# Who makes the second step addition: GpSimd in every bundle of the current round, and the instruction order laid down anew

## The chip, the cores and the metric

The kernel runs on one core of one Trainium2 chip. The metric is the time of one execution in device microseconds (us). The kernel before took 698.04 us as the median of three runs (697.25 to 698.42). The execution that the profiler recorded took 698.16 us; from its first to its last instruction, which is called the span, it is 696.4 us, at a granted TensorE clock of 1.000.

## The reference, cut to what matters

Two attention blocks work on the same input `x` (2048 rows, 512 columns), and a gate for each row mixes them. Block A is softmax attention with 32 heads of 16 columns; block B is linear attention.

```python
q, k, v = qkv[0], qkv[1], qkv[2]                       # block A, per head
scores = jnp.einsum("bhqd,bhkd->bhqk", q, k) * (Dh ** -0.5)
p = _softmax(scores, axis=-1)
o = jnp.einsum("bhqk,bhkd->bhqd", p, v)
...
phi = lambda t: jnp.where(t > 0, t + 1, jnp.exp(t)) + 1e-6   # block B
...
return g * a + (1 - g) * b                             # g = sigmoid((x * gate_w).sum(-1))
```

What costs is the exponential of block A: 32 heads x 2048 x 2048 scores.

## The kernel before, in words

**Units and rounds.** The scores are cut into units of 128 keys x 512 queries of one head; a unit fills one PSUM bank (128 x 512 float32). One round is a set of four heads and one block of 512 queries: 64 units. There are 32 rounds, so 2048 units in all. Each head set's K, V and Q projections, block B, and the output products are cut into steps that are spread between the rounds.

**Two ways to the exponential.** Most units go to ScalarE (`ACTIVATE`, L1999), which takes two or three neighbouring banks at a time (a *group*) and writes bf16 to the tile `PT`. The others are *claimed* for VectorE: L1536 turns the score into an int16 whose bits, read as a float16, are a coarse power of two (tile `DP`). Four claimed units make a *bundle*. A bundle is sharpened by a sum of three such powers, shifted by steps of 0, 342 and 683 in the int16: so each bundle needs two *step additions* over 128 x 2048 int16, from one `DP` buffer to another. VectorE makes them in L1585. For some bundles GpSimd makes the second one instead (L1578, as 128 x 1024 int32 with a pair of step values in each word). The condition stands in `try_close`: the bundle's number must divide by `EVERY`, all of its units must lie in the round that ScalarE is at (`act_round`), the round must not be the last, and over `POOL_LEFT` = 22 of the round's units must not have been claimed. GpSimd also makes the normalisation of most head blocks (`OT`, L1265).

**Products.** TensorE makes the products with V in sets of four matmuls of 32 columns each. A unit on ScalarE is one product (`PT,Vaug`); a bundle of VectorE is twelve (`DP,Vaug`, four units x three shifts).

**What sets the order.** Nothing is scheduled on the chip. A Python loop (`while True:`, with `g` as the number of the group) lays down the order of every engine's instructions once, with clocks of its own for each engine (`PE.t`, `AC.t`, `DV.t`, `PO.t`), estimated durations (`d_act`, `d_sb`, `d_psum`, `POOL_ADD` = 1.97) and constants such as `OVER`, `STARVE`, `LEND`. Every engine then runs its own queue in order, and waits at semaphores. For each group the loop takes two or three units from `next_unit`; if it takes two, the third bank of the slot may carry a claimed unit (`claim_in_group`), so that three score matmuls are issued together. Then it fills TensorE's time until the next group with products (`pv_step`), with projection or output steps (`misc_step`), with claims that stand alone, or with *fills* (`warm`, matmuls on zeros that only keep TensorE busy). VectorE's and GpSimd's pending work is kept in `items` and is laid down by `pump` and `pool_go`. In `est_start` the loop keeps a VectorE operation that reads no PSUM out of the estimated running time of a GpSimd operation (`pool_runs`).

**Banks.** PSUM has eight banks. Banks 0 to 2 and 3 to 5 are two slots (`SLOTS`) in which the groups alternate, bank 6 or 7 holds the accumulator of the products, and the other one (`MISC`) the steps. A third bank of a slot can be lent to a step when the steps are far behind (`LEND`, `lent`).

Lines that the prediction speaks of: L664 (every matmul is recorded under this helper's line), L948 (exponential of block B on ScalarE), L1277 (VectorE copies the accumulator out at a round's end), L1250 (reciprocal of the row sums, which waits for a DMA), L1293 and L1294 (the last round's normalisation).

Of the kernel before, what the change touches and what calls it, by code (L numbers as in the profile page):

```python
# [212 lines left out]
def bass_gated_mix__mha_block__linear_attn_block__prompt_kernel(  # L213
# [29 lines left out]
    PRE_T = 5  # L243
    PRE_GAP = 6
    OUT_GAP = 8

    with ExitStack() as es:
# [193 lines left out]
        POOL_ADD = 1.97  # L441
        EVERY = 2
        POOL_LEFT = 22
# [219 lines left out]
        def f_mm(o, l, r, start=True, stop=True, sg=False):  # L663
            return lambda: nc.tensor.matmul(o, lhsT=l, rhs=r, start=start, stop=stop, skip_group_check=sg)  # L664
# [824 lines left out]
        MIN_LEFT = 14  # L1489
        MIN_LEFT_LAST = 20  # L1490

# [59 lines left out]

        LAZY = 1
        MOST_ADDS = 20
        MOST_OPEN = 0
        CLAIM_FREE_OPEN = 2

        def try_close():

            while closing:
# [7 lines left out]
                if len(free) < (LAZY if early else 1):  # L1567
                    return False
                if not zs and sum(1 for it in items if it.prio == 3) >= (1 if early else MOST_ADDS):
                    return False  # L1570
# [144 lines left out]
        def behind_by():  # L1715

            return max([cur_g[0] - ch[0].target for ch in chains if ch] or [0])
# [23 lines left out]
        def misc_step(now, t_late):  # L1741
# [9 lines left out]
            if b is None:  # L1751
                return False
            due, load = due_step(now)
# [12 lines left out]
        def fill(now):  # L1766
# [17 lines left out]
            return True  # L1784

        HURRY = 40
        CLAIM_FREE = 2
        FORCE_N = 1
        MOST = 3
        OVER = 0.15  # L1790
        FIRST_T = 0.43
        ROOM = 0.4
        CLAIM_LOAD = 3.7
        LATE_CLAIM = 4
        STARVE = 6.0
        MAC_LOW = 0.45
# [141 lines left out]
        while True:  # L1938
# [7 lines left out]
            if g > last_stage and lent[0] is None and hold[0] is None and (behind_by() > LEND or (e_chain and LEND_E)) and bank_free(PE.t + 0.3) is None:  # L1946
                due, _ = due_step(PE.t + 0.3)
                if due is not None and not due[0].keeps:
                    lend = due
            while len(us) < SLOTS[g % 2][1]:  # L1950
                if len(us) == 2 and (away or lend is not None):
                    break
                if len(us) == 2 and g > last_stage:
                    extra = claim_in_group(PE.t, [j for j in range(4) if j not in [u % 4 for _, u in us]])
                    if extra is not None:
                        break
                u = next_unit()
                if u is None:
                    break
                us.append(u)  # L1960
# [31 lines left out]
            pe_macro(fns, reads=rd, writes=[r_bank[b0 + k] for k in range(len(fns))], dur=QK_T, mac=0.053 * len(fns), mode="rows")  # L1992
            if extra is not None:
                claim(extra[0], extra[1], b0 + 2, True, in_group=True)
# [18 lines left out]
            nb0, nbn = SLOTS[(g + 1) % 2]  # L2013
            if lent[0] == nb0 + 2:
                nbn = 2
# [269 lines left out]
```

## Time and profile before

| | |
|---|---|
| runs | 698.04 us, median of 3 (697.25 to 698.42) |
| profiled execution | 698.16 us; span 696.4 us |
| ScalarE busy | 682.6 us in 707 instructions |
| TensorE busy | 672.9 us in 8162 matmuls |
| VectorE busy | 641.6 us in 1099 instructions |
| GpSimd busy | 139.6 us in 91 instructions |

A busy share is how much of the span at least one instruction of that engine was on record. Consecutive instructions of an engine overlap in the record: the next starts while the one before still drains. So a wait that is shorter than the drain doesn't show as idle time, and what one more instruction costs is the distance from start to start, not its recorded duration. In a row of groups, `xcount | busy, mean ns of one | idle before` follow the operation, its tiles and its shape; behind the arrow stands what ended the idle time.

### The profile page before, as it was taken

The numbers are of one execution on the slowest core, as the hardware profiler recorded it, in microseconds if no ns is written. First come the engines' busy times: TensorE is split into PE (matmuls) and PEld (weight loads), VectorE is DVE, ScalarE is ACT, GpSimd is POOL, SyncE is SP. The second block draws the span as 40 slices with busy tenths as digits, with TensorE's granted clock in tenths as the row PEclk, the third lists the DMA queues.
The fourth block names the chain that finished last, engine by engine and source line by source line (L and its number), as shares of the span: only waits on it lengthen the run. The fifth ranks groups of instructions, "written<-read, shape, count | busy, mean of one in ns | idle before, by whom it ended". The sixth has DMA issues, their size and how long they took to land.

```text
span 696.4 us, 19208 instructions
## 1 busy us (share of the span) xinstructions
PE 672.9 (97%) x8162; PEld 203.7 (29%) x8164; DVE 641.6 (92%) x1099; ACT 682.6 (98%) x707; POOL 139.6 (20%) x91
## 2 busy tenths in 40 slices
PE   8999999999999999999999999999999999999997
PEld 4322223232223222333222323323222322222223
DVE  4699999999999999988999999999999999999894
ACT  6999999999999999999999999999999999999996
POOL 4012122121122231112211212232212320312200
PEclk9999999999999999999999999999999999999999
DMA  9800001000010001201001020010211121010121
GB/s 228 230 3 15 20 2 33 2 19 18 5 30 2 18 18 38 52 5 34 2 10 25 19 38 10 17 26 4 46 17 28 38 41 48 9 41 17 26 48 34
DMA packets 44816, 22.96 MB, mean 33 GB/s; under 512 B 33976, under 2 KB 40568, under 8 KB 44728
## 3 DMA queue, kind: packets, MB, share of 16 engines
q1 hardware_dynamic: 42712, 20.12, 12.7%
q10 hardware_dynamic: 2016, 1.57, 0.8%
q8 instruction: 67, 1.10, 0.7%
q14 instruction: 21, 0.17, 0.1%
HBM read 8.00 MB, written 2.10 MB: 14 GB/s over the span
## 4 chain that ended last, share of the span: by engine, by line
ACT 85%; PE 13%; DVE 0%; issue 0%; POOL 0%; ACTq 0%; POOLq 0%
ACT PT L1999 83%; PE ps L664 13%; ACT epool L948 2%; PE ps L671 0%; DVE DP L2095 0%; DVE xT L1867 0%; DVE KT L837 0%; DVE DP L2100 0%; DVE flag L2105 0%; POOL warm L712 0%; POOL dummy L681 0%; ACT eg L932 0%; POOL step L713 0%; ACTq L2208 0%; POOLq L2270 0%
## 5 line engine op out<-in xcount | busy, mean ns | idle before, releaser
L1999 ACT ACTIVATE PT<-ps 128x1024 bf16<-128x1024 f32 (+1 forms) x667 | 674.0, 1324 | 1.4 <-PE ps L664 1.3
L1536 DVE TENSOR_SCALAR DP<-ps 128x512 int16<-128x512 f32 x596 | 391.8, 683 | 24.0 <-PE ps L664 19.9
L664 PE MATMUL ps<-Qpad,KT 32*128 32x512 bf16 x2048 | 269.5, 384 | 16.4 <-ACT PT L1999 12.0
L664 PE MATMUL ps<-DP,Vaug 128*32 128x512 f16 x1779 | 203.4, 385 | 0.4 <-DVE DP L1536 0.2
L1578 POOL TENSOR_TENSOR DP<-DP,step 128x1024 int32<-128x1024 int32 x59 | 115.2, 1952 | 438.3 <-DVE DP L1536 336.5
L664 PE MATMUL ps<-PT,Vaug 128*32 128x512 bf16 x1435 | 176.8, 385 | 0.9 <-DVE oraw L1277 0.5
L1585 DVE TENSOR_SCALAR DP<-DP 128x2048 int16<-128x2048 int16 x239 | 159.3, 687 | 0.0
L664 PEld LDWEIGHTS ps<-Qpad,KT 32*128 32x128 bf16 x2048 | 66.8, 91 | 283.4 <-ACT PT L1999 258.6
L664 PEld LDWEIGHTS ps<-DP,Vaug 128*32 128x32 bf16 x1779 | 48.7, 94 | 62.9 <-issue 37.6
L664 PE MATMUL ps<-warm 128*32 128x512 bf16 (+1 forms) x463 | 61.8, 385 | 1.1 <-POOL step L713 1.1
L664 PEld LDWEIGHTS ps<-PT,Vaug 128*32 128x32 bf16 x1435 | 42.5, 94 | 56.2 <-issue 44.8
L1265 POOL TENSOR_TENSOR OT<-oraw,rbc 128x512 bf16<-128x512 f32 x12 | 16.0, 1334 | 76.7 <-DVE DP L1585 41.7
L664 PE MATMUL ps<-xT,wA 128*32 128x512 bf16 x432 | 31.0, 383 | 0.0
L948 ACT ACTIVATE epool<-ps 128x512 bf16<-128x512 f32 x32 | 26.8, 836 | 0.0
L1277 DVE COPY oraw<-ps 128x512 f32<-128x512 f32 x31 | 21.1, 680 | 0.3 <-PE ps L664 0.3
L664 PEld LDWEIGHTS ps<-warm 128*32 128x32 bf16 (+1 forms) x463 | 16.1, 97 | 13.2 <-issue 9.8
L664 PE MATMUL ps<-wB,xT 128*32 128x512 bf16 x256 | 19.3, 384 | 0.2 <-DVE OBT L953 0.2
L664 PE MATMUL ps<-xT,wB 128*32 128x512 bf16 x256 | 18.8, 383 | 0.0
L664 PE MATMUL ps<-woA,OT 128*32 128x512 bf16 (+1 forms) x226 | 18.7, 383 | 0.0
L953 DVE SCALAR_TENSOR_TENSOR phi<-ps,epool 128x512 bf16<-128x512 f32 x24 | 16.3, 680 | 0.0
L837 DVE CAST KT<-ps 128x512 bf16<-128x512 f32 (+1 forms) x16 | 10.6, 664 | 5.2 <-PE ps L664 5.2
L664 PE MATMUL ps<-wA,xT 128*128 128x128 bf16 x192 | 14.4, 220 | 0.0
(106 smaller groups left out, 246.5 us busy)
## 6 DMA issues: line engine op xcount, KB each, us to landing
rbc<-oraw SPq DMA_DIRECT2D x16, 256.0 KB
OT<-in_A_x_dram SPq DMA_DIRECT2D x4, 512.0 KB, 7.6
Qpad<-Qs SPq DMA_DIRECT2D x124, 16.0 KB, 1.8
oraw<-oraw SPq DMA_DIRECT2D x60, 32.0 KB, 2.0
wA<-in_A_wqkv_dram SPq DMA_DIRECT2D x1, 1536.0 KB, 8.5
wB<-in_B_wqkv_dram SPq DMA_DIRECT2D x1, 1536.0 KB, 9.1
out_dram<-outt SPq DMA_DIRECT2D x12, 128.0 KB, 1.7
phi<-in_A_x_dram ACTq DMA_DIRECT2D x3, 256.0 KB, 6.1
```

The costliest lines, as they stand in the source:

```text
L664: return lambda: nc.tensor.matmul(o, lhsT=l, rhs=r, start=start, stop=stop, skip_group_check=sg)
L837: push(1, [(lambda: nc.vector.tensor_copy(KT[:, par, c0:c1], src), [r_bank[b]], [r_KT[par][t]], d_psum(n), None)])
L948: op(AC, lambda: nc.scalar.activation(epool[:, s, :], bank_ap(b), ACT.Exp), reads=[r_bank[b]], writes=[r_e[s]], dur=0.6, issue=0.48)
L953: (lambda: nc.vector.scalar_tensor_tensor(out=dst, in0=bank_ap(b), scalar=0.0, in1=epool[:, s, :], op0=ALU.max, op1=ALU.add), [r_bank[b], ...
L1265: push(1, [(lambda: (nc.gpsimd if on_pool else nc.vector).tensor_tensor(OT[:, t8, 512 * qc:512 * (qc + 1)], oraw[:, 0, :], rbc[:], ALU.mul ...
L1277: push(0, [(lambda: nc.vector.tensor_copy(oraw[:, half, :], acc), [r_acc], [r_oraw[half]], d_psum(512), evicted)])
L1536: push(0 if in_group else 1, [(lambda: nc.vector.tensor_scalar(DP[:, i, 512 * k:512 * (k + 1)].bitcast(I16), bank_ap(b), FRAC - Y_BIAS4, Y ...
L1578: push(3, [(lambda z=z, i2=i2, y=DP[:, i, 0:n].bitcast(I32), n=n: nc.gpsimd.tensor_tensor(DP[:, i2, 0:n].bitcast(I32), y, step2[:].bitcast ...
L1585: push(3, [(lambda z=z, i2=i2, y=y, n=n: nc.vector.tensor_single_scalar(DP[:, i2, 0:n].bitcast(I16), y, STEPS[z], ALU.add), mine_, out_, d ...
L1999: op(AC, lambda p0=p0, b0=b0, n=n: nc.scalar.activation(PT[:, 512 * p0:512 * p0 + n], ps[:, 512 * b0:512 * b0 + n], ACT.Exp, scale=LN2 / F ...
```

## The change

The title's first part is one constant: `EVERY` goes from 2 to 1, so GpSimd takes the second step addition of each bundle that meets the other conditions, not of every other one. The second part is several edits of the loop: a step may be started in the third bank of a slot when the steps are over `THIRD` = 30 groups behind (`misc_step`); a group's third score may go to another free bank than the slot's third (`eb`), and the next group waits at most `WAIT3` = 0.2 us for its third bank where it waited for all three; after the staged start a group has a third unit for ScalarE only if the slot's own third bank is free and nothing can be claimed. Seven constants are changed besides. As the order is laid down from the estimates, any of these edits shifts nearly every instruction behind it.

```diff
-    PRE_GAP = 6
-    OUT_GAP = 8
+    PRE_GAP = 8
+    OUT_GAP = 4
...
-        EVERY = 2
+        EVERY = 1
...
-        MIN_LEFT_LAST = 20
+        MIN_LEFT_LAST = 18
...
-                return False
+                if behind_by() <= THIRD or lent[0] is not None:
+                    return False
+                due, load = due_step(now)
+                if due is None or due[0].keeps or now + FIRST_T > t_late + OVER:
+                    return False
+                b3 = next((b for b in (2, 5) if is_free(b, now)), None)
+                if b3 is None or not is_free(7 - b3, t_late + WAIT3):
+                    return False
...
+                start_step(due[0], b3)
+                return True
...
+        WAIT3 = 0.2
+        THIRD = 30
-        OVER = 0.15
+        OVER = 0.12
-        STARVE = 6.0
+        STARVE = 7
-        LEND = 120
+        LEND = 900
-        LATE = 8
+        LATE = 7
...
+            eb = None
+            if g > last_stage:
+                soon = PE.t + WAIT3
+                eb = next((b for b in (b0 + 2, 7 - (b0 + 2)) if is_free(b, soon)), None)
+                if eb is None and not reserved() and hold[0] is None and due_step(PE.t)[0] is None:
+                    eb = bank_free(PE.t + 0.02)
             while len(us) < SLOTS[g % 2][1]:
...
+                if len(us) == 2 and g > last_stage and eb is None:
+                    break
                 if len(us) == 2 and g > last_stage:
                     extra = claim_in_group(PE.t, [j for j in range(4) if j not in [u % 4 for _, u in us]])
-                    if extra is not None:
+                    if extra is not None or eb != b0 + 2:
                         break
...
-                fns.append(f_mm(RINGB[b0 + 2], kt, q))
+                fns.append(f_mm(bank_ap(eb), kt, q))
...
-            if lent[0] == nb0 + 2:
+            if lent[0] == nb0 + 2 or g + 1 > last_stage:
                 nbn = 2
...
+            b3 = nb0 + 2
+            if g + 1 > last_stage and b3 not in bank_busy and lent[0] != b3:
+                if r_bank[b3].pend:
+                    pump(t_lim)
+                if not r_bank[b3].pend:
+                    t_lim = max(t_lim, min(t_lim + WAIT3, r_bank[b3].tr + LAT))
```

What comes out of it can be counted in the order in which each kernel issues its instructions (the branch for rare inputs, which is not run here, left out):

| | before | after |
|---|---|---|
| units claimed for VectorE (L1536) | 596 (149 bundles) | 612 (153 bundles) |
| step additions on VectorE | 239 | 190 |
| step additions on GpSimd | 59 | 116 |
| units on ScalarE | 1452 | 1436 |
| groups on ScalarE of two, three and one banks | 547, 119, 1 | 598, 80, 0 |
| exponentials of block B on ScalarE | 32 | 32 |
| product matmuls `DP,Vaug` and `PT,Vaug` | 1815, 1503 | 1851, 1469 |
| fill matmuls (`warm`) | 463 | 381 |
| product sets with a wait for GpSimd | 58 | 112 |
| DMAs on SyncE | no change in number and kind | |

More of the change, by code (lines that the diff above doesn't have):

```diff
@@ L1552, in bass_gated_mix__mha_block__linear_attn_block__prompt_kernel @@
         LAZY = 1
+        EARLY_ADDS = 1
         MOST_ADDS = 20
@@ L1568, in try_close @@
                     return False
-                if not zs and sum(1 for it in items if it.prio == 3) >= (1 if early else MOST_ADDS):
+                if not zs and sum(1 for it in items if it.prio == 3) >= (EARLY_ADDS if early else MOST_ADDS):
                     return False
@@ L1751, in misc_step @@
             if b is None:
-                return False
+                if behind_by() <= THIRD or lent[0] is not None:
[6 more added lines that the diff above has]
+                    return False
+                STATS["thirds"] = STATS.get("thirds", 0) + 1
+                due[1].popleft()
+                start_step(due[0], b3)
+                return True
             due, load = due_step(now)
@@ L1989, in bass_gated_mix__mha_block__linear_attn_block__prompt_kernel @@
                 kt, q, rr = unit_aps(*extra)
-                fns.append(f_mm(RINGB[b0 + 2], kt, q))
+                fns.append(f_mm(bank_ap(eb), kt, q))
                 rd += [res for res in rr if res not in rd]
-            pe_macro(fns, reads=rd, writes=[r_bank[b0 + k] for k in range(len(fns))], dur=QK_T, mac=0.053 * len(fns), mode="rows")
+            pe_macro(fns, reads=rd, writes=[r_bank[b0 + k] for k in range(len(us))] + ([r_bank[eb]] if extra is not None else []), dur=QK_T, mac=0.053 * len(fns), mode="rows")
             if extra is not None:
-                claim(extra[0], extra[1], b0 + 2, True, in_group=True)
+                claim(extra[0], extra[1], eb, True, in_group=True)
                 STATS["in_group"] = STATS.get("in_group", 0) + 1
```

## The prediction

> **What bounds the kernel now.** I first read the page: which engine is busy, in which stretches, and what the chain that ended last is made of.
>
> ```profile
> span 696.4 us, 19208 instructions
> PE 672.9 (97%) x8162; PEld 203.7 (29%) x8164; DVE 641.6 (92%) x1099; ACT 682.6 (98%) x707; POOL 139.6 (20%) x91
> ...
> ACT  6999999999999999999999999999999999999996
> ...
> PEclk9999999999999999999999999999999999999999
> ...
> ACT 85%; PE 13%; DVE 0%; issue 0%; POOL 0%; ACTq 0%; POOLq 0%
> ```
>
> ScalarE is busy for 682.6 of 696.4 us, at nine tenths or more in every slice but the first and the last. The chain lies 85% on it; where it runs over TensorE (13%), the two engines follow one another closely. TensorE is nearly as busy, but some of that is fill. So the time is the start of the exponentials, their number times the distance between them, what ScalarE waits in between, and the tail. For the distance I read the chain in order of time, where one kind of instruction stands alone:
>
> ```profile
> 172.59 0.49 ACT epool L948
> 173.09 5.50 ACT PT L1999 x6
> ...
> 179.07 6.42 ACT PT L1999 x7
> ```
>
> Six two-bank exponentials take 5.50 us, seven 6.42: 0.917 us each. A one-bank exponential takes 0.49. A bank thus costs 0.917 - 0.49 = 0.427 us, and a group 0.49 - 0.427 = 0.063 us on top. That a third bank costs as much as the second is my assumption. Now the groups, one row for each form:
>
> ```profile
> L1999 ACT ACTIVATE PT<-ps 128x1024 bf16<-128x1024 f32 x547 | 532.0, 1254 | 0.8 <-PE ps L664 0.8
> L1999 ACT ACTIVATE PT<-ps 128x1536 bf16<-128x1536 f32 x119 | 182.5, 1650 | 0.7 <-PE ps L664 0.5
> L948 ACT ACTIVATE epool<-ps 128x512 bf16<-128x512 f32 x32 | 26.8, 836 | 0.0
> L1999 ACT ACTIVATE PT<-ps 128x512 bf16<-128x512 f32 x1 | 0.9, 886 | 0.0
> ```
>
> That is 547 x 2 + 119 x 3 + 1 = 1452 banks in 667 groups: 1452 x 0.427 + 667 x 0.063 = 662.0 us. With 32 x 0.49 = 15.7 for block B it is 677.7 us. The first exponential and the work behind the last one are in these rows:
>
> ```profile
> 9.84 7.16 ACT L1999 ACTIVATE PT<-ps 128x1536 bf16<-128x1536 f32 x5 [0.53 <-PE ps L664]
> ...
> 688.97 0.67 PE ps L664 x20
> ```
>
> From 9.84 to 688.97 are 679.1 us, so 1.4 us are left for waits over all groups. The tail is 696.4 - 689.0 = 7.4 us, and 698.16 - 696.4 = 1.8 us lie around the span. Hence ScalarE's work is the time, nearly to the microsecond.
>
> **The change part by part.**
>
> *ScalarE.* In the order of the changed kernel 612 units are claimed for VectorE, not 596, so ScalarE has 1436 banks, in 598 groups of two and 80 of three: 678 groups. It saves 16 x 0.427 = 6.8 us of banks and pays 11 x 0.063 = 0.7 us for more groups: **-6.1 us**. Nothing else of ScalarE's changes in number. All of it lies on the path.
>
> *VectorE.* It is what pays for the 16 units:
>
> ```profile
> L1536 DVE TENSOR_SCALAR DP<-ps 128x512 int16<-128x512 f32 x596 | 391.8, 683 | 24.0 <-PE ps L664 19.9
> ...
> L1578 POOL TENSOR_TENSOR DP<-DP,step 128x1024 int32<-128x1024 int32 x59 | 115.2, 1952 | 438.3 <-DVE DP L1536 336.5
> ...
> L1585 DVE TENSOR_SCALAR DP<-DP 128x2048 int16<-128x2048 int16 x239 | 159.3, 687 | 0.0
> ```
>
> A claim keeps VectorE for 391.8 / 596 = 0.657 us, a step addition for 159.3 / 239 = 0.667. It loses 49 additions (-32.7 us) and gains 16 claims (+10.5 us): 22 us less, 641.6 to about 619.4. Off the path this is worth nothing by itself; it is room for copying scores out of PSUM in time.
>
> *GpSimd.* 57 more additions of 1.952 us are 111 us more, 139.6 to about 251 of some 690 us. That fits: there is a bundle every 680 / 153 = 4.4 us, and an addition takes 1.95 of them. But a sum is then ready 1.952 - 0.687 = 1.27 us later than from VectorE, and the product sets that have a wait for GpSimd grow from 58 to 112. What those waits cost stands here:
>
> ```profile
> PEld ps L664 <- ACT PT L1999: 258.6, 578, 1.0
> ...
> PEld ps L664 <- POOL DP L1578: 2.0, 7, 0.4
> ```
>
> TensorE waited 7 times for GpSimd, 2.0 us in all, 0.4 at most; and 578 times for ScalarE to free a bank, 258.6 / 578 = 0.45 us each. A late product is paid out of that 0.45, as behind it in TensorE's queue stand the next scores, which can't start before the bank is free anyway. Doubled (4 us) the waits would still be within the cover, so I cost them at nothing; without the cover, all of it would be ScalarE's.
>
> *ScalarE's waits.* The largest wait before shows how they come about:
>
> ```profile
> 448.92 0.35 DVE L1250 RECIPROCAL rraw<-rsum 128x32 f32<-128x32 f32 x1 [0.98 <-DMA rsum<-oraw]
> ...
> 449.19 1.90 DVE L1536 TENSOR_SCALAR DP<-ps 128x512 int16<-128x512 f32 x3
> ...
> 449.93 0.13 PEld L664 LDWEIGHTS ps<-Qpad,KT 32*128 32x128 bf16 x3 [0.91 <-ACT PT L1999]
> ...
> 450.39 1.94 ACT L1999 ACTIVATE PT<-ps 128x1024 bf16<-128x1024 f32 x2 [0.57 <-PE ps L664]
> ```
>
> A reciprocal stood 0.98 us at the head of VectorE's queue for a DMA; the claims behind it left their banks late; the next three scores, of which one uses such a bank, started late; ScalarE stood still. More room on VectorE and the 0.2 us limit on waiting for the third bank work against such chains; the denser GpSimd additions, each of which keeps VectorE's work within SBUF apart, and 11 more groups, each with a hand-over of its own, work for them. I can't weigh the two by rows. The bounds are all 1.4 us gone, or growth with GpSimd's additions, 116 / 59, again and again: twice is 2.8 us. I take the latter, **+1.4**, since the additions are what this change has most of.
>
> *Tail.* Before, the last exponential is one bank; after, two, which drains 1.25 - 0.89 = 0.37 us later, while its step is in the sum above. Behind it come 8 small products, not 20 (0.67 us, so 0.27): -0.4. Then seven output matmuls, not four, stand on TensorE ahead of the transposes that wait for the last normalisation:
>
> ```profile
> 689.68 0.26 DVE L1293 RECIPROCAL rraw<-ps 128x16 f32<-128x16 f32 x1 [4.70 <-PE ps L664]
> 689.70 0.81 PE L664 MATMUL ps<-woB,OBT 128*128 128x512 bf16 x3
> ...
> 690.45 0.40 PE L671 MATMUL ps<-identb,Osb 128*128 128x128 bf16 x4
> ```
>
> Three of them ended 0.81 us after the first began, one drain of 0.38 within: 0.21 each. Seven take 1.5 us, where 0.8 lay between the products' end and the transposes: +0.7, less the 0.4 that an earlier start would bring at best. With the drain I take **+0.3** (0 to +0.7).
>
> *The rest.* Fills fall from 463 to 381 matmuls; they take time in which TensorE has nothing else. The DMAs are the same in number and kind; only their place moves. Output steps are laid 4 groups apart, not 8: 12 of them in the last rounds, on TensorE beside the exponentials. I cost these at nothing.
>
> **Sum:** 698.16 - 6.1 + 1.4 + 0.3 = 693.8 us, 4.4 less than the profiled execution, which stands 0.1 us above the median.
>
> **The rivals.** *A, the gain is eaten on VectorE: no change.* An addition on VectorE that starts while GpSimd works within SBUF stands still to its end:
>
> ```profile
> 247.48 1.27 POOL L1265 TENSOR_TENSOR OT<-oraw,rbc 128x512 bf16<-128x512 f32 x1 [5.07 <-DMA rbc<-oraw]
> 247.56 1.74 DVE L1585 TENSOR_SCALAR DP<-DP 128x2048 int16<-128x2048 int16 x1
> ...
> L1585 DVE TENSOR_SCALAR DP<-DP x239: 628/682/1736, 34.8 to 683.7; 128x2048 int16<-128x2048 int16 x120
> ```
>
> It took 1.74 us, not the median 0.68: it ran from the end of GpSimd's operation on. If half of the 57 new additions caught one like it, VectorE would lose 28 x 1.06 = 30 us, more than the 22 it gained; it would be as full as now, the copies as late, and each late copy would pay back part of the 6.1 us: about 698. Against it: the mean of VectorE's additions is 687 ns at a median of 682, so with 71 GpSimd operations such cases cost 239 x 0.005 = 1.2 us in all, and nothing of ScalarE's idle time stands there. [...]
>
> *B, late sums hold TensorE: slower.* TensorE's queue is in order. A product set that comes 1.27 us too early for its sum stands for that time, and beyond the 0.45 us of cover ScalarE pays 0.82. From the sixth such set the gain of 4.4 is gone; were it one in eight of the 112, 14 x 0.82 = 11.5 us, the time would be 705. A like place is GpSimd's queue: its `OT` operation stood at the head until a DMA had landed, and additions stand behind it.
>
> ```profile
> POOL OT L1265 <- DMA rbc<-oraw: 34.9, 5, 8.8
> ```
>
> Against it: 7 of 58 waited, and none beyond the cover. For it: GpSimd sat idle between most additions, and so the trace shows none that stood behind another for long.
>
> *C, better: the room on VectorE counts.* The 1.4 us of waits go and none come: 698.2 - 6.1 - 1.4 + 0.3 = 691.0.
>
> *D, the change does not do what it says.* The count of claims is certain, so only the distance between exponentials could: were a three-bank group cheaper than I assume, by 0.03 us, giving 39 of them up costs 1.2 us more, within the range.
>
> **How the numbers follow.** The sum with its bounds (698.16 - 6.1 = 692.1 with neither waits nor tail added, 695.6 with 2.8 and 0.7) 0.62; C 0.10; A 0.14; B 0.12; anything else 0.02. The range takes the sum, C and A, from 690.6 to 698.4, which holds about 0.85 and leaves out B. Within 0.2% (about what a measurement of this kernel can tell from no change; 1.4 us) lies most of A; faster are the sum, C and the edge of A. Faster 0.74, same 0.13, slower 0.13.
>
> **What would show it.** Right: ScalarE's groups at 0.917 us a step with some 3 us of waits in all, VectorE busy near 619 us, GpSimd near 251, TensorE's waits for GpSimd near 4 us with none over 0.45. Wrong by A: VectorE's additions with a mean well over 687 ns. Wrong by B: single waits of TensorE for GpSimd of 0.8 us or more, and ScalarE idle behind them. Wrong otherwise: a distance between exponentials that isn't 0.917, or a clock below 1.00.

## The result, and the profile after

The changed kernel takes **693.76 us**, the median of six runs (691.92 to 694.27). The kernel before, run beside it, takes 698.18 us (697.25 to 698.58, six runs). The ratio is 0.9936, 95% interval 0.9925 to 0.9946: 4.4 us less. The execution that the profiler recorded took 693.24 us, with a span of 691.4 us at a granted clock of 1.0.

The page of the changed kernel, in the order in which the page of before was read. `L2021` is the exponential that was L1999, `L1586` the step addition on VectorE, `L1579` the one on GpSimd.

```profile
span 691.4 us, 19104 instructions
...
PE 670.5 (97%) x8082; PEld 203.0 (29%) x8084; DVE 624.7 (90%) x1066; ACT 677.6 (98%) x718; POOL 249.6 (36%) x148
...
ACT  6999999999999999999999999999999999999996
...
PEclk9999999999999999999999999999999999999999
...
ACT 80%; PE 15%; DVE 4%; issue 0%; POOL 0%; ACTq 0%; POOLq 0%
...
L1536 DVE TENSOR_SCALAR DP<-ps 128x512 int16<-128x512 f32 x612 | 401.7, 683 | 38.1 <-PE ps L664 34.5
L1579 POOL TENSOR_TENSOR DP<-DP,step 128x1024 int32<-128x1024 int32 x116 | 225.9, 1947 | 349.2 <-DVE DP L1586 220.0
...
L1586 DVE TENSOR_SCALAR DP<-DP 128x2048 int16<-128x2048 int16 x190 | 127.4, 686 | 0.2
```

ScalarE is still the bound: 98% of the span, nine tenths or more in every slice but the ends. GpSimd's busy time went up by 110 us, VectorE's down by 16.9 us, and of that room VectorE now spends 38.1 us (24.0 before) waiting for scores to copy (`L1536`, the last column but one). The claims cost what they cost before, 401.7 / 612 = 0.656 us, and so do the additions, 127.4 / 190 = 0.671.

ScalarE's groups in the form-by-form view of the changed kernel, then its chain in order of time (start, length, what) at the place where two-bank exponentials stand alone, and the first ones in the timeline:

```profile
L2021 ACT ACTIVATE PT<-ps 128x1024 bf16<-128x1024 f32 x598 | 568.0, 1167 | 1.1 <-PE ps L664 0.9
L2021 ACT ACTIVATE PT<-ps 128x1536 bf16<-128x1536 f32 x80 | 118.9, 1585 | 0.7 <-PE ps L664 0.5
```

```profile
178.01 0.49 ACT epool L948
178.50 6.42 ACT PT L2021 x7
...
685.49 0.39 PE ps L671 x4
```

```profile
9.12 4.27 ACT L2021 ACTIVATE PT<-ps 128x1536 bf16<-128x1536 f32 x3 [0.53 <-PE ps L664]
...
677.09 6.54 ACT L2021 ACTIVATE PT<-ps 128x1536 bf16<-128x1536 f32 x5
```

Seven two-bank groups again take 6.42 us, 0.917 each, and one bank 0.49. The third bank, whose price the prediction assumed, can be read off the trace: from the start of a three-bank group to the start of the next exponential the median is 1.331 us (1.330 in before), from a two-bank group 0.904 in both, so a third bank costs 0.427 or 0.426. So the price list of the prediction holds for the second kernel, and the account by it is 598 x 2 + 80 x 3 = 1436 banks x 0.427 + 678 groups x 0.063 = **655.9 us** where before it was 662.0, and 671.6 with block B. The recorded means fell (1254 to 1167 ns) although the distance did not: the record of one exponential overlaps the next more or less, and only the distance from start to start is a price.

What ScalarE waited in all comes from the two ends. The last two-bank exponential ends at 677.09 + 6.54 = 683.63; in the trace it began at 682.41. From 9.12 to 682.41, plus its own step of 0.92, are 674.2 us; less 671.6 are **2.6 us of waits**, where the same reckoning gives 688.97 - 9.84 - 677.7 - 0.4 = 1.0 for before. (The prediction had 1.4, as it took the last exponential to its recorded end; 0.89 - 0.49 = 0.4 us of that is drain, which here belongs to the tail.) The tail from the end of that last step to the end of the span is 691.4 - 683.3 = 8.1 us; before, 7.9.

The waits on TensorE's queue and ScalarE's own (who for whom, us, times, longest); the prediction had named those for GpSimd for rival B:

```profile
PEld ps L664 <- ACT PT L2021: 252.4, 582, 1.4
...
PEld ps L664 <- POOL DP L1579: 2.7, 11, 0.4
ACT PT L2021 <- PE ps L664: 1.4, 4, 0.5
```

There are collisions of rival A's kind in the trace, operations of VectorE that last until one of GpSimd's has ended. The longest is in the timeline of the changed kernel at 64 us, where two instructions start 10 ns apart:

```profile
64.28 1.89 POOL L1579 TENSOR_TENSOR DP<-DP,step 128x1024 int32<-128x1024 int32 x1 [2.27 <-DVE DP L1536]
64.29 2.04 DVE L951 TENSOR_SCALAR epool<-epool 128x512 bf16<-128x512 bf16 x1
...
66.25 0.68 DVE L1536 TENSOR_SCALAR DP<-ps 128x512 int16<-128x512 f32 x1
...
67.51 1.02 ACT L2021 ACTIVATE PT<-ps 128x1024 bf16<-128x1024 f32 x1 [0.50 <-PE ps L664]
...
68.70 1.02 ACT L2021 ACTIVATE PT<-ps 128x1024 bf16<-128x1024 f32 x1 [0.17 <-PE ps L664]
```

VectorE's `L951` takes 2.04 us. Its median is 0.28, in the first of these rows (shortest, median, longest in ns); the second is that of the step additions:

```profile
L951 DVE TENSOR_SCALAR epool<-epool x32: 281/283/2035, 36.7 to 524.0; 128x512 bf16<-128x512 bf16 x32
...
L1586 DVE TENSOR_SCALAR DP<-DP x190: 628/682/1424, 34.1 to 677.2; 128x2048 int16<-128x2048 int16 x190
```

`L951` ended 0.15 us after GpSimd's addition, the claim behind it left its bank late, and ScalarE stood 0.50 and 0.17 us. Two more operations were caught for over 0.3 us: `L951` at 176.8 us (0.65 us) behind an addition, and an addition of VectorE's at 208.2 us (the 1424 of the second row) behind GpSimd's `L1265`. Behind these two no step of ScalarE is more than 0.35 us longer than the median of its kind. GpSimd's addition at 64.28 us, which started 10 ns earlier, ran its usual 1.89 us, and `L951` waited it out. The other way round it is GpSimd that is longer: 16 of its 116 additions started 0.05 to 0.17 us into an addition of VectorE's, which took its usual 0.68 to 0.70 us, and these 16 took 2.27 to 2.40 us where the other 100 took 1.89 to 1.90.

### The profile page after: what moved, and what is told of

It reads as the page before. It is cut to its first block, busy times and chain, and to the rows that moved or that the text cites. A ratio compares the mean times of both kernels' runs of the same rounds, so it can differ in the third digit from the quotient of the medians.

```text
span 691.4 us, 19104 instructions
## 1 busy us (share of the span) xinstructions
PE 670.5 (97%) x8082; PEld 203.0 (29%) x8084; DVE 624.7 (90%) x1066; ACT 677.6 (98%) x718; POOL 249.6 (36%) x148
## 4 chain that ended last, share of the span: by engine, by line
ACT 80%; PE 15%; DVE 4%; issue 0%; POOL 0%; ACTq 0%; POOLq 0%
ACT PT L2021 78%; PE ps L664 15%; ACT epool L948 2%; DVE DP L1536 2%; DVE DP L1586 1%; DVE epool L951 0%; DVE DP L2123 0%; DVE oraw L1277 0%; DVE xT L1881 0%; DVE phi L953 0%; DVE KT L837 0%; PE ps L671 0%; DVE OB L1076 0%; DVE DP L2128 0%; DVE flag L2133 0%
## 5 line engine op out<-in xcount | busy, mean ns | idle before, releaser
L2021 ACT ACTIVATE PT<-ps 128x1024 bf16<-128x1024 f32 (+1 forms) x678 | 666.5, 1216 | 1.8 <-PE ps L664 1.4
L1536 DVE TENSOR_SCALAR DP<-ps 128x512 int16<-128x512 f32 x612 | 401.7, 683 | 38.1 <-PE ps L664 34.5
L1579 POOL TENSOR_TENSOR DP<-DP,step 128x1024 int32<-128x1024 int32 x116 | 225.9, 1947 | 349.2 <-DVE DP L1586 220.0
L664 PE MATMUL ps<-Qpad,KT 32*128 32x512 bf16 x2048 | 273.7, 384 | 12.7 <-ACT PT L2021 8.2
L664 PE MATMUL ps<-DP,Vaug 128*32 128x512 f16 x1831 | 199.9, 384 | 1.3 <-DVE oraw L1277 0.9
L664 PEld LDWEIGHTS ps<-Qpad,KT 32*128 32x128 bf16 x2048 | 68.6, 91 | 278.8 <-ACT PT L2021 250.5
L1586 DVE TENSOR_SCALAR DP<-DP 128x2048 int16<-128x2048 int16 x190 | 127.4, 686 | 0.2
L664 PEld LDWEIGHTS ps<-DP,Vaug 128*32 128x32 bf16 x1831 | 48.4, 94 | 65.1 <-issue 37.7
L664 PE MATMUL ps<-warm 128*32 128x512 bf16 (+1 forms) x381 | 56.3, 385 | 1.1 <-POOL step L713 1.1
L1265 POOL TENSOR_TENSOR OT<-oraw,rbc 128x512 bf16<-128x512 f32 x12 | 15.3, 1274 | 56.4 <-DMA rbc<-oraw 28.6
L948 ACT ACTIVATE epool<-ps 128x512 bf16<-128x512 f32 x32 | 24.2, 756 | 0.0
L1277 DVE COPY oraw<-ps 128x512 f32<-128x512 f32 x31 | 21.1, 681 | 0.6 <-PE ps L664 0.5
L664 PEld LDWEIGHTS ps<-warm 128*32 128x32 bf16 (+1 forms) x381 | 14.3, 97 | 15.0 <-issue 12.0
```

What stands on the lines that cost most here:

```text
L948: op(AC, lambda: nc.scalar.activation(epool[:, s, :], bank_ap(b), ACT.Exp), reads=[r_bank[b]], writes=[r_e[s]], dur=0.6, issue=0.48)
L1265: push(1, [(lambda: (nc.gpsimd if on_pool else nc.vector).tensor_tensor(OT[:, t8, 512 * qc:512 * (qc + 1)], oraw[:, 0, :], rbc[:], ALU.mul ...
L1277: push(0, [(lambda: nc.vector.tensor_copy(oraw[:, half, :], acc), [r_acc], [r_oraw[half]], d_psum(512), evicted)])
L1536: push(0 if in_group else 1, [(lambda: nc.vector.tensor_scalar(DP[:, i, 512 * k:512 * (k + 1)].bitcast(I16), bank_ap(b), FRAC - Y_BIAS4, Y ...
L1579: push(3, [(lambda z=z, i2=i2, y=DP[:, i, 0:n].bitcast(I32), n=n: nc.gpsimd.tensor_tensor(DP[:, i2, 0:n].bitcast(I32), y, step2[:].bitcast ...
L1586: push(3, [(lambda z=z, i2=i2, y=y, n=n: nc.vector.tensor_single_scalar(DP[:, i2, 0:n].bitcast(I16), y, STEPS[z], ALU.add), mine_, out_, d ...
```

## The experiments

**Theory T:** the time is ScalarE's work as the order has it (banks x 0.427 + groups x 0.063) plus a rest of 36 to 38 us; so the gain comes from the 16 more claims. The rest is the measured time less that sum: 698.2 - 662.0 = 36.2 before, 693.8 - 655.9 = 37.9 after. **Rivals:** the GpSimd part alone brings the gain, by the room on VectorE (G); the loop alone brings it (L); the two rest on the scheduling itself, not on the counts (S); and the prediction's A and B as costs that hide in the result. The counts of every kernel below come from the order of its instructions. Where a kernel's waits and tail are given, they are worked out from its trace as for the changed kernel above. Four sets of kernels ran, each with runs of the kernel before beside it (697.86, 697.72, 697.67 and 697.67 us).

### The first part alone (e1)

```diff
 (kernel before)
-        EVERY = 2
+        EVERY = 1
```

> The kernel before with EVERY = 1 and nothing else: the GpSimd part of the change alone. Its order has 110 additions on GpSimd and 186 on VectorE (before: 59 and 239), but only 592 claims (596), so ScalarE has 1456 banks in 685 groups (1452 in 667). Theory T (the time is ScalarE's banks and groups, 0.427 us and 0.063 us each; what VectorE or GpSimd gain counts only where it becomes a claim): 664.9 us of such steps where before has 662.0, so 2.9 us slower than before, about 701 us, if the waits stay as they are, 702 with 1.4 us more of them. Rival G (a less loaded VectorE pays by itself, through fewer and shorter waits): faster than before, 695 to 697 us.

704.09 us (703.69 to 704.32), ratio 1.009 (1.0075 to 1.0105): **slower**. Its page:

```profile
PE 682.5 (97%) x8071; PEld 206.4 (29%) x8073; DVE 613.4 (87%) x1042; ACT 686.7 (98%) x725; POOL 237.9 (34%) x142
```

VectorE has less work than in any other kernel here, 28 us less than before, and the time is 6 us longer. G falls: room on VectorE is worth nothing unless the loop turns it into claims, and here the old loop claimed 592 units, four fewer. Sum 664.9, 2.9 more than before; the rest is 39.2, 3 us above before's, so T has the sign and half of the size. The other half is ScalarE's waits: by its trace they are 4.2 us, where before has 1.0. Whether the denser additions or the order make them is not shown.

### The second part alone (e2)

```diff
 (kernel after)
-        EVERY = 1
+        EVERY = 2
```

> The kernel after with EVERY = 2 again: the edits of the loop without the GpSimd part. Its order has 56 additions on GpSimd, 238 on VectorE, 588 claims, 1460 banks in 668 groups. Theory T: 665.5 us of steps, 3.5 us more than before: 701.7 us, less what the shorter wait for the third bank saves (under 1.4 us, all that ScalarE waits before). Rival L (the edits of the loop are what made the kernel faster, GpSimd's part is for nothing): 693 to 695 us.

701.61 us (701.09 to 702.1), ratio 1.0057 (1.0043 to 1.0071): slower as well.

```profile
PE 675.5 (97%) x8134; PEld 204.7 (29%) x8136; DVE 636.1 (91%) x1090; ACT 686.3 (98%) x708; POOL 134.2 (19%) x88
```

588 claims, sum 665.5, rest 36.1. T hit it within 0.1 us; L falls. Neither part gains alone, and together, in the order of after, they do. Whether that is a rule or an accident of one order, the other kernels below that have both parts, and some edit of the loop besides, can hint at. Leaving out the one without the gate (e4), the sums of the seven different orders are 653.0, 654.5, 655.7, 655.9 (after), 661.0, 661.3 and 665.0 us: six of seven lie under the 662.0 of before, and one is about as high as either part alone (664.9 and 665.5). So the pair tends to leave ScalarE fewer banks, but a single order can lose all of it; and as each part alone was laid down once, that the gain belongs to the pair as a rule is not shown. The sum is a count, not a time: it shows work, not waits.

### GpSimd's additions made short, same order (e3)

```diff
 (kernel after, L1579)
-  y=DP[:, i, 0:n] ... DP[:, i2, 0:n] ... [128, n // 2]
+  y=DP[:, i, 0:4] ... DP[:, i2, 0:4] ... [128, 2]
```

It leaves out the second shift of those 116 bundles, for all but two of 1024 words in a row. (GpSimd also clears the `DP` buffers once at the start, in 11.2 us.)

> The kernel after in the same order on every engine, but each of GpSimd's 116 step additions covers 2 of 1024 columns; GpSimd also clears the DP buffers once at the start. Left out is the second shift of those bundles. [...] Theory T: the waits that came with denser additions go, 693.8 less 1 to 3 us, so 691 to 693 us. Rivals A and B (additions on GpSimd that stop VectorE, or come late for TensorE, eat a good part of what they bring): 5 us or more come back, under 689 us.

692.12 us (691.61 to 692.36), ratio 0.9919 (0.9905 to 0.9932). The order, the claims and what waits for what are those of after; only the additions are short. A group of its view, and `epool` by tile (its lines stand one lower):

```profile
L1580 POOL TENSOR_TENSOR DP<-DP,step 128x2 int32<-128x2 int32 x116 | 29.0, 250 | 511.0 <-DVE DP L1587 335.8 <-DVE DP L1537 175.2
...
L952 DVE TENSOR_SCALAR epool<-epool x32: 281/283/407, 36.6 to 522.5; 128x512 bf16<-128x512 bf16 x32
```

The rest is 36.2, as in the kernel before. So **the length of GpSimd's additions costs this order 693.76 - 692.12 = 1.6 us** (1.2 by the ratios, as the two kernels ran in different sets), A and B together, and the collision of 2.04 us is gone (longest 0.41). Rivals A and B, which had 5 us or more coming back, fall for this order. What the gate costs through the order that it forces is not in this number.

Where the time is lost can be read from the two traces, since ScalarE's instructions are the same in number and order. The thin kernel's exponentials start 0.2 us earlier than after's at 59 us, 1.4 us earlier at 106 us, and 1.5 us earlier at the end. So 1.2 of the 1.3 us that it gains from the first exponential to the last is gained in one place, and the steps that shorten there are those at 65.7, 67.5 and 71.0 us, right behind the collision of `L951`.

### The gate that keeps VectorE out of GpSimd's time, taken away (e4)

```diff
 (kernel after, emit_item_op)
-                pool_runs.append((PO.t - on_pool[0] + 0.08, PO.t + 0.08))
```

> The kernel after, but the loop no longer keeps VectorE's work within SBUF out of the estimated running time of a GpSimd operation. The order comes out with 618 claims, 198 and 110 additions, 1430 banks in 672 groups: 652.9 us of steps, 3.0 less than after. [...] Rival A (VectorE's fast operation and GpSimd's shut each other out for a whole operation): with 198 additions and GpSimd at work a third of the time some 60 of VectorE's operations are caught, for about 1 us each; VectorE, with some 50 us idle, carries part of that, and ScalarE pays the rest: slower than after, 697 to 710 us.

731.4 us (728.99 to 732.81), ratio 1.0483 (1.0463 to 1.0503), although the loop, which sees no gate, claims 618 units and the sum is 652.9, the least of all, for which T says 652.9 + 37.9 = 690.8. Three rows of its page and groups:

```profile
DVE 54%; PE 31%; ACT 13%; issue 2%; POOL 0%; DVEq 0%; ACTq 0%; POOLq 0%
...
L1585 DVE TENSOR_SCALAR DP<-DP 128x2048 int16<-128x2048 int16 x198 | 174.2, 893 | 0.3
...
L2020 ACT ACTIVATE PT<-ps 128x1024 bf16<-128x1024 f32 x586 | 559.0, 1088 | 31.0 <-PE ps L663 29.0
```

The additions' mean is 893 ns, not 686: 198 x 0.207 = 41 us more on VectorE. The chain is now VectorE's (54%), and ScalarE is idle for 31 us. So A is a real mechanism. This kernel takes some 38 us more than after; in that are also stretches at half clock (mean granted clock 0.985). In after, the order keeps nearly all of it out.

### Sums laid down as if they came early (e5)

The loop is told that GpSimd's sum is there 1.27 us sooner than it will be, so it lays the products down too early:

```diff
 (kernel after, emit_item_op, behind _emit(PO, ...))
+                if on_pool[0] == POOL_ADD:
+                    for res in writes:
+                        res.tw -= 1.27
```

> The kernel after, but the loop believes that a sum from GpSimd is ready 1.27 us before it estimates the end of the addition (so as early as one from VectorE); the times in which it keeps VectorE apart are as before. The order comes out with 600 claims, 113 and 187 additions, 1448 banks in 678 groups: 661.0 us of steps, and 106 product sets wait for GpSimd. Theory T with the rest as after (693.8 - 655.9 = 37.9 us): 698.9 us, and TensorE's waits for GpSimd grow from 2.7 us to some tens, but within the cover of 0.45 us each. Rival B (a sum that comes 1.27 us too late for a product at the head of TensorE's queue costs ScalarE 0.82): with half of the 106 sets at the head at once 40 us more, about 740 us; with one in eight 710.

723.48 us (721.47 to 724.16), ratio 1.0361 (1.0347 to 1.0374). Sum 661.0, so T says 698.9 and misses by 24.6. The waits of this kernel, and its chain:

```profile
PEld ps L667 <- POOL DP L1582: 43.8, 55, 1.2
PE ps L667 <- POOL DP L1582: 27.5, 41, 0.9
...
ACT PT L2024 <- PE ps L667: 18.9, 40, 1.1
```

```profile
PE 34%; ACT 31%; DVE 21%; POOL 10%; issue 2%; SPq 1%; DMA 0%; DVEq 0%; ACTq 0%; POOLq 0%
```

TensorE's weight loads stood 55 times for GpSimd, up to 1.2 us (in after 11 times, up to 0.4), and 40 of ScalarE's groups began late. ScalarE's waits are 27.5 us by the trace, 24.9 more than in after, which is the miss. B is real too: late sums cost 25 us as soon as the order doesn't allow for them. In after it does.

### One constant of the loop back (e6)

```diff
 (kernel after)
-        WAIT3 = 0.2
+        WAIT3 = 0.1
```

> The kernel after with WAIT3 = 0.1 in place of 0.2: the same two parts, but the order laid down has 591 claims, 108 and 186 additions, 1457 banks in 680 groups: 665.0 us of steps. Theory T: 665.0 + 37.9 = 702.9 us, slower than the kernel before although the change is made. Rival S (it is what the change does to each bundle that counts, and the order is about as good either way): 693 to 696 us.

702.36 us (702.29 to 703.95), ratio 1.0067 (1.0054 to 1.008). Claims fall to 591, the sum is 665.0, the rest 37.4. Nearly the same scheduling with other counts is slower than before, by what the counts say: S falls, T holds.

### More claims (e7)

```diff
 (kernel after)
-        POOL_ADD = 1.97
+        POOL_ADD = 1.9
...
-        MIN_LEFT = 14
+        MIN_LEFT = 10
```

> The kernel after with POOL_ADD = 1.9 (the profile's GpSimd additions mostly take 1.89 us) and MIN_LEFT = 10. The order has 619 claims, 126 and 182 additions, 1429 banks in 679 groups: 653.0 us of steps. Theory T: 653.0 + 37.9 = 690.9 us, faster than both kernels; with 10 more additions on GpSimd up to 0.3 us more. Rival A (the shorter estimate of GpSimd's running time lets VectorE's work run into it): the 2.9 us are eaten, 693 to 696 us.

619 claims, sum 653.0, T: 690.9. Measured **699.3** (697.32 to 700.82, twelve runs), ratio 1.0019 (1.0007 to 1.003). T misses by 8.4, and rival A, at 693 to 696, by over 3. The timeline of this kernel has a collision again, of other instructions:

```profile
477.67 1.89 POOL L1579 TENSOR_TENSOR DP<-DP,step 128x1024 int32<-128x1024 int32 x1 [0.86 <-DVE DP L1586]
...
478.43 1.64 DVE L903 TENSOR_SCALAR Vaug<-Vaug 128x576 bf16<-128x576 bf16 x2
...
480.13 1.04 PE L664 MATMUL ps<-DP,Vaug 128*32 128x512 f16 x8 [2.41 <-DVE Vaug L903]
...
481.76 1.94 ACT L2021 ACTIVATE PT<-ps 128x1024 bf16<-128x1024 f32 x2 [2.78 <-PE ps L664]
```

`L903` prepares V for the next products. The first of the two came 0.76 us into GpSimd's addition, stood to its end and took 1.30 us, not the usual 0.30. TensorE, whose next products needed it, was idle for 2.41 us, of which about 1.0 is thus the collision's. What came of that is in the view by stretches (busy us and count of PE, PEld, DVE, ACT, POOL; then the granted clock):

```profile
476.00:478.00 2.00, 1.72 (x22) 0.67 (x19) 1.78 (x5) 2.00 (x3) 1.14 (x2) 1.00 0.15 33
478.00:480.00 2.00, 0.00 (x0) 0.00 (x0) 1.93 (x4) 0.98 (x1) 1.56 (x1) 0.78 0.09 8
480.00:482.00 2.00, 1.87 (x15) 0.28 (x15) 0.91 (x3) 0.24 (x1) 0.00 (x0) 0.50 0.13 29
...
486.00:488.00 2.00, 2.00 (x16) 0.32 (x15) 1.64 (x3) 1.51 (x2) 0.80 (x1) 0.50 0.00 0
488.00:489.00 1.00, 1.00 (x12) 0.22 (x8) 0.32 (x1) 0.51 (x2) 0.00 (x0) 0.50 0.00 0
...
490.00:491.00 1.00, 1.00 (x18) 0.27 (x14) 1.00 (x2) 1.00 (x2) 0.88 (x1) 1.00 0.00 0
```

The granted clock fell to 0.50 and stayed there until after 489 us, although TensorE was busy again from 480.1 us on. At half clock the scores came late and ScalarE worked 1.51 of 2 us. So one gap of TensorE's, made longer by a collision, and the half clock behind it cost ScalarE some 5 us. The rest is in four other places. ScalarE's waits in this execution are 11.2 us by the trace, 8.6 more than in after, and at 332, 370, 610 and 654 us single steps of ScalarE are 1.2 to 1.4 us longer than usual. At 370 it is `L951` again, caught behind `L1265` for 1.41 us. The other three are ends of rounds, where TensorE waits for VectorE to copy the accumulator out (`L1277`); first the row of this kernel, then of after:

```profile
PE ps L664 <- DVE oraw L1277: 3.8, 6, 0.9
...
PE ps L664 <- DVE oraw L1277: 1.2, 3, 0.5
```

The tail is 1.7 us longer than after's besides. Why this order has its copies late is not shown.

### A wider gate (e8)

```diff
 (kernel after, emit_item_op)
-                pool_runs.append((PO.t - on_pool[0] + 0.08, PO.t + 0.08))
+                pool_runs.append((PO.t - on_pool[0] + 0.08, PO.t + 0.4))
```

> The kernel after, but VectorE's work within SBUF is kept out for 0.32 us more behind each GpSimd operation. The order has 600 claims, 109 and 191 additions, 1448 banks in 682 groups: 661.3 us of steps. Theory T: the rest falls from 37.9 us to that of the kernel with thin additions (692.1 - 655.9 = 36.2), as hardly an operation is caught any more: 697.5 us, no better than before. Rival (the waits of after come from something else than caught operations): 699 us, and as many caught operations as in after.

700.92 us (699.98 to 701.03), ratio 1.004 (1.0027 to 1.0053); 600 claims, sum 661.3, rest 39.6. T, which counted on hardly an operation being caught, has the direction and misses by 3.4 us; its rival (699, and as many caught) is nearer. Against after, by the trace, the first exponential starts about 0.9 us later, the waits are about 0.9 us longer and the tail 0.7. A later end of the gate does not help with what starts at the same time as GpSimd's addition: the collision of `L951` is there still, now at 65.1 us, 2.03 us long.

### GpSimd made to wait for VectorE (e9, e10, e11)

GpSimd's operation waits in addition for the last VectorE operation without PSUM that was laid down ahead of it. First with the order of after, then with that of the kernel with more claims, then with `OVER` = 0.15 (0.12), which gives 615 claims:

```diff
 (kernel after, _emit)
+            if behind is not None and behind[0] is not None:
+                st = max(st, behind[1] + LAT)
-            ev = E.add(fn, _deps_for(reads, writes), inc=inc)
+            ev = E.add(fn, _deps_for(reads, writes) + ([behind[0]] if behind is not None else []), inc=inc)
+            if E is DV and not any(res in r_bank for res in reads):
+                last_sb[:] = [ev, st + dur]
```

> The kernel after, in the same order on every engine; each GpSimd operation also waits for the last VectorE operation within SBUF that was laid down ahead of it. So GpSimd can no longer start just before such an operation and shut it out; it can still run into one that was laid down behind it. Theory T (the rest of 37.9 us holds 1 to 2 us that caught operations cost): the catch at 64 us goes, 692 to 693 us. Rival (operations are caught since VectorE is early, not since GpSimd is): no change, 693.8 us, with the same catches.

> The kernel of e7_more_claims in the same order, with the wait of e9_pool_behind. That kernel had 653.0 us of steps but took 699.3 us: an operation caught at 478 us left TensorE idle for 2.4 us, its granted clock then fell to 0.50 until 490 us, and ScalarE lost over 5 us there. Theory T: with the caught operations gone the rest is that of after or less, 653.0 + 36.2 to 37.9 = 689.2 to 690.9 us, the clock stays at 1.00. Rival (the order itself has ScalarE wait, and the caught operations are only where it shows): 695 us or more.

> The kernel of e9_pool_behind with OVER = 0.15 as before the change. Its order has 615 claims, 118 and 188 additions, 1433 banks in 676 groups: 654.5 us of steps. Theory T: 690.7 to 692.4 us. Rival (the step sum says little, as what an order loses in waits differs by several us from one order to the next): anywhere from 692 to 700 us.

693.14 us (691.89 to 694.35), 699.29 (697.24 to 702.67, twelve runs) and 693.32 (692.83 to 693.51); ratios 0.993 (0.9917 to 0.9943), 1.0027 (1.0012 to 1.0041), 0.9939 (0.9926 to 0.9952). The first kernel's 693.14 against after's 693.76 lies within the spread, so the wait gains nothing that can be told from it. Its rival, which had the same operations caught, is right, as the view by tile shows:

```profile
L957 DVE TENSOR_SCALAR epool<-epool x32: 281/283/2034, 36.8 to 525.2; 128x512 bf16<-128x512 bf16 x32
```

The longest is still 2034 ns. The operations that get caught are laid down *behind* GpSimd's in the order, by an estimate that has them start after it; a wait for what is laid down ahead can't reach them. The same holds for the second kernel: the operation that was `L903` is caught at 479.3 us for 1.30 us as in e7, the clock halves behind it (here for 3.4 us), and the time is that of e7, 8 us over T's range and where its rival had it. The third kernel has three claims more than after and a sum lower by 1.4 us, and is no faster: its rest is 38.8, of which the tail in its trace has 0.8 us more than after's (8.9 against 8.1). Its time lies 0.9 us above T's range.

### A margin at the gate's front (e12)

```diff
 (kernel after, emit_item_op)
-                pool_runs.append((PO.t - on_pool[0] + 0.08, PO.t + 0.08))
+                pool_runs.append((PO.t - on_pool[0] + 0.08 - 0.5, PO.t + 0.08))
```

> The kernel after, but the times in which the loop keeps VectorE's work within SBUF apart begin 0.5 us ahead of the estimated start of a GpSimd operation, not at it. The order comes out with 612 claims, 114 and 192 additions, 1436 banks in 675 groups: 655.7 us of steps, like after (655.9). The operations that were caught in after and again in e9_pool_behind were laid down behind GpSimd's, to start at nearly the same time. Theory T: they are no longer caught, the rest falls from 37.9 us towards that of the kernel with thin additions (36.2), so 692 us. Rival (the rest differs from order to order by chance, and the caught operations are a small part of it): 693 to 695 us, even with none caught.

719.84 us (719.13 to 720.15), ratio 1.0319 (1.0305 to 1.0333). 612 claims, sum 655.7, the same as after; rest 64.1. Neither T nor its rival had that. `L951` is at most 297 ns now; but two slices of ScalarE's row and the timeline show a new thing:

```profile
ACT  6999999999999999899999999999999999999920
```

```profile
680.98 5.22 ACT L2021 ACTIVATE PT<-ps 128x1536 bf16<-128x1536 f32 x4
...
691.75 0.75 DVE L1141 TENSOR_SCALAR outt<-ps,gom 128x512 bf16<-128x512 f32 x1 [2.02 <-PE ps L664]
...
694.52 0.75 DVE L1141 TENSOR_SCALAR outt<-ps,gom 128x512 bf16<-128x512 f32 x1 [2.02 <-PE ps L664]
...
712.70 0.69 ACT L2117 ACTIVATE DP<-ps,gom 128x512 bf16<-128x512 f32 x1 [26.50 <-PE ps L664]
```

The last exponential ends at 686.2 us, and then output steps that found no place between the groups follow one another, 2.77 us each, while ScalarE waits 26.5 us. T's sum is blind to work that is left over behind the last exponential. Up to there, this kernel needs 686.2 us where after needs 683.6; its clock is at 0.50 for 3.4 us from 102.8 us on and for 6.8 us from 290.6 us on, and ScalarE's longest waits are there and at 475 us. So nothing is shown for or against the margin itself; an order with it and without left-over steps was not tried.

## Why the prediction was right

The forecast was 693.8 us; measured are 693.76. That the two agree to 0.04 us is luck, as the six runs scatter from 691.92 to 694.27. That the gain is near 4.4 us is not: its largest term was counted and priced. By its own steps, in the profiled executions (696.4 to 691.4, -5.0):

| step | predicted | measured |
|---|---|---|
| ScalarE's banks and groups | -6.1 | -6.1 by count, the distances of 0.917 and 0.49 are unchanged |
| ScalarE's waits | +1.4 | +1.6 (2.6 against 1.0); by e3, 1.3 of the waits are due to the additions' length |
| tail | +0.3 | +0.2 |
| first exponential | 0 | -0.7 (9.12 against 9.84) |

- **ScalarE.** Right, and tested by undoing either part: the kernel with the new loop alone came out within 0.1 us of what its counts give, the one with `WAIT3` back 0.5 us below. The prediction took a third bank's price on trust; the trace has it at 0.427, so giving up 39 three-bank groups hides no error (the prediction's D).
- **ScalarE's waits.** This was the part with the weakest ground, "growth with GpSimd's additions". The size is right, but by luck: it came from doubling 1.4 us of waits in the ratio of the additions, and before has 1.0 by the reckoning above. That the additions' length is the cause is shown: with them short, and the order as it was, ScalarE's waits are 1.3 us, near the 1.0 of before. The mechanism was another one than forecast. The prediction has growth with each addition, "again and again"; the traces of after and e3 differ in one place, behind the collision at 64.3 us, which makes some 1.2 us. That is what rival A describes, once and at an operation that the prediction did not look at. The spread growth that was forecast did not show.
- **VectorE.** Busy 624.7, not 619.4. The prices of a claim and an addition were right (0.656, 0.671); of the 5 us, 4.4 are overlap: the durations of VectorE's instructions sum to 21.4 us less than before, but consecutive ones overlap by 4.4 us less. Off the path, as said: 14 us more idle time before the claims.
- **GpSimd.** 249.6 against 251; 1947 ns against 1952.
- **TensorE's waits for GpSimd.** 2.7 us in 11 waits, longest 0.4, against "near 4, none over 0.45". They were costed at nothing, and GpSimd has 0% of the chain.
- **Rival A** (no change): an addition on VectorE takes 686 ns in the mean, so it did not come to pass there; one addition was caught (1.42 us), as one had been before. But the prediction looked only at the additions, and what cost ScalarE time was another operation, `L951`. e4, without the gate, has 41 us more on VectorE's additions; the prediction's estimate of half of the new ones caught (30 us on VectorE) was of the right kind.
- **Rival B** (slower): e5 shows that it would have cost 25 us. The prediction set its chance by the 7 of 58 waits before; that row was the right one, since it says that the order allows for GpSimd's duration.
- **The start** was not forecast. The first exponential came 0.7 us sooner. In the profiled executions of all these kernels it starts anywhere from 8.9 to 10.0 us, so whether this is the change or the execution stays open. The forecast is 0.6 us above the profiled execution's 693.24, and this is the reason: without the -0.7 the two small misses, +0.2 and -0.1, leave the forecast 0.1 us below it.
- **What stays open.** The rest varies from 36 to 39.6 us between orders. The traces say which part of it grew (waits in e1; start, waits and tail in e8; tail in e11), but no run shows why these orders have it and others do not. In e1 ScalarE's waits grew by 3.2 us, in e7 by 8.6, so the prediction's bound of 2.8 us held for the order at hand and is none for others.

## What to carry to other kernels

When one engine is full from end to end, count its instructions in the new order and price them by the distance from start to start; with the rest of the nearest kernel that gave four of the variants here to 1 us (e2, e6, e9, e11) and two to 3.4 us (e1, e8), and it failed where operations were caught (e4), sums came late (e5), TensorE ran dry and waited at ends of rounds (e7, e10), or work was left over behind the last exponential (e12). Relieving an engine off the path earns only what the scheduler turns into less work for the bound engine: each half of this change alone made the kernel slower, and so did both together with one constant of the loop set otherwise (e6). Then look for the single places where two engines shut each other out at the same moment: one of them, with the half clock behind it, cost some 5 us of ScalarE's in e7, as much as the 4.4 us that this whole change gained.

## What the hardware showed that was not expected

**A short idle gap, half the clock for up to ten microseconds.** In the kernel with more claims (e7) TensorE was idle for 2.4 us from 477.7 us on. By the clock record of its trace the granted clock fell to 0.50 at 479.1 us, 1.4 us into that gap, and came back at 489.3 us, with TensorE on record as busy in all of it from 480.1 us on. In the profiled execution of e9 it fell at 69.0 us, for 3.4 us; the longest idle time of TensorE between 62 and 69 us is 1.11 us, up to 67.16 us, behind the collision of `L951`. The profiled execution of after has the same 1.11 us at the same place, up to 67.07 us, and its clock stayed at 1.00 until 690.9 us, 0.5 us before its end. The falls lasted 10.2 us in e7, 3.4 in e9 and in e10, 3.4 and 6.8 in e12. So in e7 the clock fell within an idle gap, in e9 1.8 us behind the end of a shorter one, and in after not at all behind one as short; what decides it is not shown. Nor is it shown whether the fills, which keep TensorE busy, prevent such falls: no run here leaves them out.

**The same race falls the same way.** `L951` and GpSimd's addition started 10 ns apart or less, and the collision stands in the profile of after, of the kernel with the added wait (e9) and of the one with the wider gate (e8), 2035, 2034 and 2034 ns long.

**Steps of the clock in the times.** The runs of the two kernels with more claims (e7, e10) do not scatter around one value but fall into steps, and each step has its own mean granted clock: 697.2 to 697.4 us at 0.999 to 1.000, 699.2 to 699.4 at 0.996 to 0.997, 700.5 to 700.8 at 0.992 to 0.993, 702.2 to 702.7 at 0.990. The profiled run of e7, with the fall of 10.2 us, is one at 0.992; that of e10, with one of 3.4 us, is one at 0.997. So the same order meets such a drop in some executions and not in others, and from each step to the next the time is 1.4 to 2.0 us longer in the mean.
